# Two attention and feed-forward layers on one core: a repeated block for TensorE, other buffer slots, and the output projection at each layer's end

## The chip, the core and the metric

The kernel runs on one core of a Trainium2 chip. A core has TensorE (PE; its weight loads are shown as PEld), VectorE (DVE), ScalarE (ACT), GpSimd (POOL) and SyncE (SP), which here issues every transfer between HBM and SBUF. The engines run their own instruction streams and wait for each other on semaphores. The metric is the device time of one execution in microseconds; lower is better.

## The reference, cut to what matters

One decoding step of two layers that share their weights and their caches. B = 4 sequences, D = 512, 32 query heads in 8 groups of 4, head size 128, 8192 cached positions, feed-forward width 1792, all bfloat16.

```python
def _A_ref(x, k_cache, v_cache, wq, wo):
    q = (x @ wq)                                  # [B, 1, 32*128], by heads
    k, v = repeat(k_cache, 4), repeat(v_cache, 4) # 8 groups serve 32 heads
    scores = einsum("bhqd,bhkd->bhqk", q, k) * 128 ** -0.5
    p = softmax(scores)
    return einsum("bhqk,bhkd->bhqd", p, v) @ wo
def _B_ref(x, w_gate, w_up, w_down):
    return (silu(x @ w_gate) * (x @ w_up)) @ w_down
for _ in range(2):
    x = x + _A_ref(_layernorm(x), k_cache, v_cache, wq, wo)
    x = x + _B_ref(_layernorm(x), w_gate, w_up, w_down)
```

A cache of one sequence and group is 2 MB of keys and 2 MB of values. Both layers read all 32 of them.

## The kernel before

A *unit* is one pair of sequence and group; each layer has 32 (`NU`). SBUF holds eight slots of 2 MB (`NSLOT`) in the tensor `kvf`, and the weights `w_q` and `w_o` for good. The feed-forward weights are loaded into slots 6 and 7 (and some space behind them) at each layer's end. The last three units' keys and values of layer 1 stay in their slots, and layer 2 begins with them; so layer 2 loads 29 units.

**Transfers.** `items` lists them in order: keys of unit i, values of unit i-1, keys of unit i+1, and so on, with the parts of `w_o` in between at the start and the feed-forward weights at a layer's end. `pump` (L316) issues on SP whatever comes next while a slot is free; `finished` (L363) gives a slot back when TensorE's last read of it is written down. Any free slot may be taken. SP waits, in order, for the engines that used the slot last. In layer 2 two resident key slots are refilled in halves (`half`, L350).

**A unit.** The keys arrive with positions on partitions. `turn` (L396) lets VectorE transpose them 32 by 32 in place, in eight blocks of 128x512. `scores` (L414) multiplies each block with the placed query (`place_q`, L404, on GpSimd), four matmuls a block, into one PSUM bank. Then come a maximum (`max_p`, `max_t`, L425 to L439: VectorE, a transposing matmul, VectorE, ScalarE), the exponentials (`exps`, L441), a transposition of the probabilities (`turn_p`) and their sum (`total`). `values` (L496) multiplies the probabilities with the values in 16 matmuls of 512 columns; VectorE and ScalarE add up the diagonal blocks (`own_first`, `own_others`), a small matmul sums rows (`add_rows`, L535), and the result goes to `oT`. The last two units of a layer (`NLAST`) use 64 small matmuls instead (`block_last`, L540).

**The order.** Python code writes one order by hand for all engines: `keys` and `values` append blocks with an estimated length, `drain` keeps two microseconds of blocks behind the turns (`LAG`), and `line` and `after` hold the steps of the softmax and of the values, which `advance` lets out as time goes by. `_Sync` (L21) writes down who read and wrote what and puts a semaphore wait ahead of an instruction where needed.

**w_o.** When the four sequences of a group are done, `out_proj` (L575) is appended: 16 matmuls that gather the heads, a copy by VectorE, 16 matmuls with `w_o`, and the addition to x (`add_to_x`, L571). At a layer's end come the normalization (`center`, `deviation`), `ffn` (L647), and in the next layer `qproj` (L621).

TensorE's program is straight: every matmul of both layers stands in it, 4,700 in the built program.

Of the kernel before, what the change touches and what calls it, by code (L numbers as in the profile page):

```python
# [20 lines left out]
class _Sync:  # L21

    def __init__(self, engines, prog_sems):
        self.eng = engines
        self.prog = prog_sems
        self.count = {n: 0 for n in engines}
        self.waited = {}
        self.res = {}
        self.semval = {}

# [24 lines left out]
    def _wait(self, engname, need):  # L55
        e = self.eng[engname]
        for sem, val in need:
            k = (engname, id(sem))
            if self.waited.get(k, 0) >= val:
                continue  # L60
            if sem is self.prog.get(engname) and (val > self.count[engname] or engname == "pe"):
                continue
            e.wait_ge(sem, val)
            self.waited[k] = val

    def _record(self, engname, sv, reads, writes):
# [6 lines left out]
        for r in reads:  # L73
            rec = self.res.get(r)
            if rec is None:
                rec = self.res[r] = _Rec()
            rec.r[engname] = sv

# [25 lines left out]
def bass_interleave_layers__gqa_block_cached__swiglu_ffn__decode_kernel(  # L104
# [17 lines left out]
    REP = Hq // G  # L122
# [25 lines left out]
    with ExitStack() as es:  # L148
# [7 lines left out]
        o4 = sb("o4", [P, REP, B], BF16)  # L156
# [24 lines left out]
        xs = sb("xs", [P, B], FP32)  # L181
        vs = sb("vs", [P, B], FP32)
        lnv = sb("lnv", [P, B], FP32)
        rstd = sb("rstd", [P, B], FP32)
        oT = sb("oT", [P, 2, REP, B], BF16)
# [4 lines left out]
        zq = sb("zq", [P, 4, ZP + P], BF16)  # L190
# [99 lines left out]
        free = list(range(NSLOT))  # L290
        slot_of = {}

# [23 lines left out]
        def pump():  # L316
            while issued[0] < len(items):
                n = issued[0]
                it = items[n]
                if it[0][0] == "w":  # L320
                    if it[0] == "wg":
                        if not {NKEEP, NKEEP + 1} <= set(free):
                            return
                        free[:] = [s for s in free if s < NKEEP]
# [4 lines left out]
                late = any(e - 10 < n < e for e in ends)  # L329
                fit = [s for s in free if s < NKEEP or not late]  # L330
                if not fit:
                    return
                s = fit[0] if late else max(fit, key=lambda s: s >= NKEEP)
# [29 lines left out]
        def finished(it):  # L363
# [8 lines left out]
            else:  # L372
                free.append(slot_of[it])
# [22 lines left out]
        def turn(L, u, q):  # L396


            s = slot_of["K", L, u]
            w = kv[:, s, q * TB * Dh:(q + 1) * TB * Dh].bitcast(FP32)  # L400
            T.op("dve", lambda e: e.transpose(w, w), reads=[f"s{s}.{q}"], writes=[f"s{s}.{q}"])  # L401
            turned.add((L, u, q))

        def place_q(u, eng="pool", src=qr, keys_=SCR):  # L404
# [4 lines left out]
            dst = zq[:, :, ZP:].rearrange("p c (a x) -> p c a x", a=NA)[:, :, :, 0:REP]  # L409
# [4 lines left out]
        def scores(L, u, q):  # L414

            s = slot_of["K", L, u]
# [3 lines left out]
            for c in range(4):  # L420
                T.op("pe", lambda e: e.matmul(bank(bk)[:, 0:SW], lhsT=zq[:, c, z0:z0 + P], rhs=w[:, :, c // 2, :, c % 2],  # L421
                                              start=(q == 0 and c == 0), stop=(q == NB - 1 and c == 3)),
                     reads=[f"s{s}.{q}", "zq"], writes=[f"pb{bk}"], sig=(c == 3))
# [6 lines left out]
        def max_t(u):  # L430
            T.op("pe", lambda e: e.matmul(bank(STEP)[0:1, 0:P], lhsT=mx[:], rhs=identf[:], is_transpose=True,  # L431
                                          start=True, stop=True),
                 reads=["mx", "ident"], writes=[f"pb{STEP}"])
# [7 lines left out]
        def exps(u):  # L441
            bk = SBK[turn_of[u]]
            T.op("pe", lambda e: e.matmul(bank(STEP)[:, 0:1], lhsT=mrow,  # L443
                                          rhs=onesf[0:1, :], start=True, stop=True),
                 reads=["pb", "onesf"], writes=[f"pb{STEP}"])
# [10 lines left out]
        def total(u):  # L456
            T.op("pe", lambda e: e.matmul(bank(TOT)[:, 0:REP], lhsT=ones, rhs=rsm[:], start=True, stop=True),  # L457
                 reads=["rsm", "onesf"], writes=[f"pb{TOT}"])
# [4 lines left out]

        blocks = []
# [8 lines left out]
        def keys(L, u):  # L473
            def block(q):
                first = u == unit_order[L][0]
                if q == 0 and not first:
# [16 lines left out]

        done = set()

        def values(L, u):  # L496
            g, b = unit_gb(u)
            bk = OBK[turn_of[u]]

# [8 lines left out]
            def block(i):  # L508
# [5 lines left out]
                for t in range(TB):  # L514
                    j = t % NA
                    c0 = t * QB + i * NV * REP
                    T.op("pe", lambda e: e.matmul(bank(bk)[j * QB:j * QB + NV * REP, :],  # L517
                                                  lhsT=pT[:, turn_of[u], c0:c0 + NV * REP], rhs=v[:, t, NV * i:NV * (i + 1), :],
                                                  start=(i == 0 and t == j), stop=(i == 1 and t >= TB - NA)),
                         reads=[f"s{s}.{NV * i + k}" for k in range(NV)] + [f"pT{turn_of[u]}"], writes=[f"pb{bk}"],  # L520
                         sig=(t == TB - 1))
# [13 lines left out]
            def add_rows():  # L535
                T.op("pe", lambda e: e.matmul(bank(LNB)[:, 0:REP], lhsT=acc[:], rhs=head[:], start=True, stop=True),  # L536
                     reads=["acc", "head"], writes=[f"pb{LNB}"])
                scale_o(LNB)

            def block_last(q):  # L540
# [6 lines left out]
                for t in range(q * TB, (q + 1) * TB):  # L547
                    c0 = (t % TB) * QB + REP * q
                    T.op("pe", lambda e: e.matmul(bank(bk)[:, 0:REP], lhsT=kv[:, s, t * Dh:(t + 1) * Dh],  # L549
                                                  rhs=pT[:, turn_of[u], c0:c0 + REP], start=(t == 0), stop=(t == TT - 1)),  # L550
                         reads=[f"s{s}.{q}", f"pT{turn_of[u]}"], writes=[f"pb{bk}"], sig=(t % TB == TB - 1))
# [3 lines left out]
            def scale_o(k):  # L555
                T.op("dve", lambda e: e.tensor_tensor(oT[:, g // (G - 1), :, b], bank(k)[:, 0:REP], rl[:, rl_of[u], :],
                                                      ALU.mult),
                     reads=[f"pb{k}", f"rl{rl_of[u]}"], writes=[f"oT{g // (G - 1)}"])
# [8 lines left out]
            if all((L, g * B + k) in done for k in range(B)):  # L567
                rest.append([0.5, None, lambda: out_proj(g)])
# [6 lines left out]
        def out_proj(g):  # L575

            pick = ident.rearrange("p (j e) -> p e j", e=REP)
            ob = bank(OUTB)[:, XB:2 * XB].rearrange("p (e b) -> p e b", b=B)
            for c in range(REP):
                for h in range(REP):  # L580
                    T.op("pe", lambda e: e.matmul(ob[h * QB:(h + 1) * QB, c, :], lhsT=pick[:, c, :],
                                                  rhs=oT[:, g // (G - 1), h, :], start=True, stop=True),
                         reads=[f"oT{g // (G - 1)}", "ident"], writes=[f"pb{OUTB}"], sig=(h == REP - 1))
            T.op("dve", lambda e: e.tensor_copy(o4[:], ob), reads=[f"pb{OUTB}"], writes=["o4"])
            for nt in range(KT):
                for c in range(REP):
                    T.op("pe", lambda e: e.matmul(bank(OUTB)[:, nt * B:(nt + 1) * B],  # L587
                                                  lhsT=wo_sb[:, g, c, nt * P:(nt + 1) * P], rhs=o4[:, c, :],
                                                  start=(c == 0), stop=(c == REP - 1)),
                         reads=[f"wo{g // (G // 4)}", "o4"], writes=[f"pb{OUTB}"], sig=(c == REP - 1))  # L590
# [6 lines left out]
        def center():  # L597
            T.op("dve", lambda e: e.tensor_reduce(xs[:], xT[:].rearrange("p (k b) -> p b k", b=B), AX.X, ALU.add),
                 reads=["x"], writes=["xs"])
            T.op("pe", lambda e: e.matmul(bank(LNB)[:, 0:B], lhsT=ones, rhs=xs[:], start=True, stop=True),  # L600
                 reads=["xs", "onesf"], writes=[f"pb{LNB}"])
# [11 lines left out]
        def deviation(bias, bkey):  # L613
            T.op("pe", lambda e: e.matmul(bank(TOT)[:, 0:B], lhsT=ones, rhs=vs[:], start=True, stop=True),
                 reads=["vs", "onesf"], writes=[f"pb{TOT}"])
            T.op("act", lambda e: e.activation(lnv[:], bank(TOT)[:, 0:B], ACTF.Ln, scale=1.0 / D, bias=eps_sb[:]),
                 reads=[f"pb{TOT}", "eps"], writes=["lnv"])
            T.op("act", lambda e: e.activation(rstd[:], lnv[:], ACTF.Exp, scale=-0.5, bias=bias[:]),
                 reads=["lnv", bkey], writes=["rstd"])

        def qproj(gs, u=None):  # L621
            h0, nh = gs[0] * REP, len(gs) * REP
            for h in range(h0, h0 + nh):
                for kt in range(KT):
                    T.op("pe", lambda e: e.matmul(bank(LNB)[:, h * B:(h + 1) * B],  # L625
                                                  lhsT=wq_sb[:, kt, h * Dh:(h + 1) * Dh],
                                                  rhs=xn[:, kt * B:(kt + 1) * B],
                                                  start=(kt == 0), stop=(kt == KT - 1)),
# [7 lines left out]
            for c in range(4):  # L636
                for a in range(NA):
                    T.op("pe", lambda e: e.matmul(ob[a * QB:(a + 1) * QB, c, :, h0:h0 + nh],
                                                  lhsT=pick[:, c // 2, :, c % 2],
                                                  rhs=qT[:, :, h0:h0 + nh], start=True, stop=True),  # L640
# [6 lines left out]
        def ffn(last):  # L647
# [5 lines left out]
            for (w_sb, wname, bk) in (([wg_sb[:, k, :] for k in range(KT)], "wg", gb), (wu_sb, "wu", ub)):  # L653
                for fo in range(FO):
# [3 lines left out]
                    for kt in range(KT):  # L658
                        T.op("pe", lambda e: e.matmul(bank(bk)[:, fo * B:(fo + 1) * B],
                                                      lhsT=w_sb[kt][:, f:f + 2 * P - 1:2],  # L660
                                                      rhs=xn[:, kt * B:(kt + 1) * B],
# [99 lines left out]
```

## Time and profile before

| | us |
|---|---|
| median of 3 runs | 655.31 (654.31 to 655.44) |
| profiled execution | 655.51 |
| its span, first to last instruction | 653.7 |
| PE busy | 500.5 (77%) |
| DVE busy | 446.1 (68%) |
| ACT busy | 116.4 (18%) |
| HBM read | 273.88 MB, 419 GB/s over the span |
| TensorE's mean granted clock | 0.824 |

A row of the profile's groups gives the line, the engine, the operation, what it writes and reads, how often, the busy time with the mean of one in ns, and the idle time of the engine ahead of it with what ended it. In the 40 slices, one is 16.3 us, and a digit is a tenth of it. "DMA" there is the mean busy share of the core's 16 DMA engines. The queue "q8 instruction" carries TensorE's program to the engine while it runs. A transfer is split over all 16 DMA engines and has landed when the last of them has done its part.

### The profile page before, as it was taken

What the parts mean: (1) busy time and instruction counts of PE and PEld (TensorE: products, weight loads), DVE (VectorE), ACT (ScalarE), POOL (GpSimd) and SP (SyncE); (2) the same over time, 40 slices, a digit from 0 to 9 for tenths busy, and PEclk for the clock granted to TensorE, in tenths of its full rate; (3) what the DMA queues carried; (4) which work ended last, traced back from release to release, by engine and by line L of the source; (5) the groups of instructions that cost most, each with busy time, mean ns of one, the idle gap of its engine ahead of it and who ended that gap; (6) DMA issues with size and microseconds to landing.
All of it is one profiled execution on the core that took longest, in us unless ns stands there. A gap on an engine that the chain in (4) does not pass through costs nothing.

```text
span 653.7 us, 11807 instructions
## 1 busy us (share of the span) xinstructions
PE 500.5 (77%) x4896; PEld 319.2 (49%) x4896; DVE 446.1 (68%) x1079; ACT 116.4 (18%) x391; POOL 19.3 (3%) x73
## 2 busy tenths in 40 slices
PE   1766787977777877787876988887688787786886
PEld 1544444544444544544555655554354454443456
DVE  2556676776776777776752399996677677676682
ACT  0021121221221221221220212221122122121120
POOL 0000000000000000000000000000000000000000
PEclk9897788777978778789685989997978887797895
DMA  9999999999999999999999999999999999999996
GB/s 368 428 425 423 438 429 427 432 431 429 430 431 429 430 430 432 430 432 428 427 416 375 398 411 431 430 428 429 430 428 429 433 430 430 432 427 429 432 420 239
DMA packets 24085, 274.64 MB, mean 420 GB/s; under 512 B 2392, under 2 KB 2400, under 8 KB 7904
## 3 DMA queue, kind: packets, MB, share of 16 engines
q1 hardware_dynamic: 24032, 273.89, 98.9%
q8 instruction: 38, 0.62, 0.3%
q14 instruction: 15, 0.12, 0.0%
HBM read 273.88 MB, written 0.00 MB: 419 GB/s over the span
## 4 chain that ended last, share of the span: by engine, by line
DMA 66%; DVE 17%; PE 13%; SPq 3%; issue 1%; ACT 0%; POOL 0%; DVEq 0%; POOLq 0%
DMA kvf<-in_A_k_cache_dram 63%; DVE kvf L401 11%; PE ps L421 8%; DVE acc L531 3%; DMA kvf<-in_B_w_down_dram 3%; SPq L93 2%; PE ps L517 1%; DVE one L427 1%; DVE pT L454 1%; PE ps L587 1%; DVE m L434 1%; PE ps L625 1%; PE ps L457 0%; PE ps L676 0%; PE ps L549 0%
## 5 line engine op out<-in xcount | busy, mean ns | idle before, releaser
L401 DVE STREAM_TRANSPOSE kvf<-kvf 128x512 f32<-128x512 f32 x488 | 322.4, 686 | 121.8 <-DMA kvf<-in_A_k_cache_dram 121.8
L421 PE MATMUL ps<-kvf,zq 128*128 128x256 bf16 x2048 | 346.2, 314 | 18.2 <-DVE kvf L401 15.7
L421 PEld LDWEIGHTS ps<-kvf,zq 128*128 128x128 bf16 x2048 | 211.3, 115 | 89.8 <-DVE kvf L401 40.4
L437 ACT ACTIVATE pb<-m 1x128 f32<-1x128 f32 x64 | 19.7, 308 | 453.5 <-DVE m L434 453.5
L431 PE MATMUL ps<-identf,one 128*1 128x128 f32 x64 | 18.3, 286 | 68.3 <-DVE one L427 68.3
L517 PE MATMUL ps<-kvf,pT 128*16 128x512 bf16 x960 | 68.5, 409 | 0.9 <-DVE rl L459 0.9
L531 DVE SCALAR_TENSOR_TENSOR acc<-ps,own,acc 128x128 f32<-128x128 f32 x180 | 63.1, 351 | 6.5 <-ACT acc L526 1.9
L431 PEld LDWEIGHTS ps<-identf,one 128*1 128x1 f32 x64 | 5.1, 80 | 99.4 <-DVE one L427 93.2
L536 PE MATMUL ps<-head,acc 128*128 128x4 f32 x120 | 26.4, 290 | 17.9 <-DVE acc L531 17.7
L536 PEld LDWEIGHTS ps<-head,acc 128*128 128x128 f32 x120 | 22.8, 237 | 34.2 <-DVE acc L531 33.6
L443 PE MATMUL ps<-one,pb 1*128 1x1 f32 x128 | 27.8, 284 | 14.1 <-ACT pb L437 13.8
L443 PEld LDWEIGHTS ps<-one,pb 1*128 1x128 f32 x128 | 22.4, 217 | 32.8 <-ACT pb L437 29.1
L449 ACT ACTIVATE pb<-ps,one,rstd 128x256 bf16<-128x256 f32 x64 | 36.2, 565 | 2.1
L412 POOL TENSOR_TENSOR zq<-scr,quad 128x64 bf16<-128x64 bf16 x62 | 18.2, 293 | 608.1 <-PE ps L421 569.4
L517 PEld LDWEIGHTS ps<-kvf,pT 128*16 128x16 bf16 x960 | 19.3, 91 | 32.8 <-issue 21.2
L427 DVE TENSOR_REDUCE one<-ps 128x1 f32<-128x256 f32 x64 | 25.6, 399 | 13.1 <-PE ps L421 12.7
L454 DVE STREAM_TRANSPOSE pT<-pb 128x256 bf16<-128x256 bf16 x64 | 25.9, 405 | 1.9 <-ACT pb L449 1.9
L457 PEld LDWEIGHTS ps<-rsm,one 128*128 128x128 f32 x128 | 24.5, 237 | 3.0 <-ACT rsm L451 0.9
L457 PE MATMUL ps<-rsm,one 128*128 128x4 f32 x128 | 21.6, 239 | 0.0
L447 ACT ACTIVATE one<-ps,rstd 128x1 f32<-128x1 f32 x64 | 16.7, 261 | 25.8 <-PE ps L443 25.8
L526 ACT ACTIVATE acc<-ps,own 128x128 f32<-128x128 f32 x60 | 20.6, 343 | 0.0
L434 DVE TENSOR_REDUCE m<-ps 1x4 f32<-1x128 f32 x64 | 15.6, 244 | 6.5 <-PE ps L431 6.5
(66 smaller groups left out, 165.9 us busy)
## 6 DMA issues: line engine op xcount, KB each, us to landing
kvf<-in_A_k_cache_dram SPq DMA_DIRECT2D x60, 2048.0 KB, 30.0
kvf<-in_A_v_cache_dram SPq DMA_DIRECT2D x58, 2048.0 KB, 33.8
wq_sb<-in_A_wq_dram SPq DMA_DIRECT2D x4, 1024.0 KB, 7.6
wo_sb<-in_A_wo_dram SPq DMA_DIRECT2D x4, 1024.0 KB, 34.5
kvf<-in_A_v_cache_dram SPq DMA_DIRECT2D x8, 512.0 KB, 19.3
kvf<-in_B_w_gate_dram SPq DMA_DIRECT2D x2, 1792.0 KB, 23.2
kvf<-in_B_w_down_dram SPq DMA_DIRECT2D x4, 768.0 KB, 16.0
kvf<-in_A_v_cache_dram SPq DMA_DIRECT2D x2, 1024.0 KB, 7.0
```

The lines of the kernel that those rows point to most:

```text
L401: T.op("dve", lambda e: e.transpose(w, w), reads=[f"s{s}.{q}"], writes=[f"s{s}.{q}"])
L421: T.op("pe", lambda e: e.matmul(bank(bk)[:, 0:SW], lhsT=zq[:, c, z0:z0 + P], rhs=w[:, :, c // 2, :, c % 2], start=(q == 0 and c == 0), sto ...
L427: T.op("dve", lambda e: e.tensor_reduce(mx[:], bank(bk)[:, 0:SW], AX.X, ALU.max), reads=[f"pb{bk}"], writes=["mx"])
L431: T.op("pe", lambda e: e.matmul(bank(STEP)[0:1, 0:P], lhsT=mx[:], rhs=identf[:], is_transpose=True, start=True, stop=True), reads=["mx", " ...
L434: T.op("dve", lambda e: e.tensor_reduce(m4[:], bank(STEP)[0:1, 0:P].rearrange("p (x h) -> p h x", h=REP), AX.X, ALU.max, negate=True), rea ...
L443: T.op("pe", lambda e: e.matmul(bank(STEP)[:, 0:1], lhsT=mrow, rhs=onesf[0:1, :], start=True, stop=True), reads=["pb", "onesf"], writes=[f ...
L449: T.op("act", lambda e: e.activation(pb[:], bank(bk)[:, 0:SW], ACTF.Exp, bias=nm[:], scale=by, accum_out=rs[:]), reads=[f"pb{bk}", "nm", " ...
L454: T.op("dve", lambda e: e.transpose(pT[:, turn_of[u], :], pb[:]), reads=["pb"], writes=[f"pT{turn_of[u]}"])
L457: T.op("pe", lambda e: e.matmul(bank(TOT)[:, 0:REP], lhsT=ones, rhs=rsm[:], start=True, stop=True), reads=["rsm", "onesf"], writes=[f"pb{T ...
L517: T.op("pe", lambda e: e.matmul(bank(bk)[j * QB:j * QB + NV * REP, :], lhsT=pT[:, turn_of[u], c0:c0 + NV * REP], rhs=v[:, t, NV * i:NV * ( ...
L531: T.op("dve", lambda e: e.scalar_tensor_tensor(acc[:], bank(bk)[:, k * Dh:(k + 1) * Dh], own[:, k:k + 1], acc[:], op0=ALU.mult, op1=ALU.ad ...
L536: T.op("pe", lambda e: e.matmul(bank(LNB)[:, 0:REP], lhsT=acc[:], rhs=head[:], start=True, stop=True), reads=["acc", "head"], writes=[f"pb ...
```

## The change

TensorE's instructions are no longer issued as they are written down. `_Sync.pe` puts them on a list with the waits that they need, and `roll` at the end looks for the longest stretch in each layer where two units repeat with the same operands and with waits whose values grow evenly. That stretch becomes a loop of TensorE alone; its waits compare with register values worked out from the turn. In the built program the loops take units 2 to 27 of layer 1 (13 turns) and units 10 to 29 of layer 2 (10 turns), counted by their place in the layer; 2,388 matmuls are left in the program. `head_slot` asks that the loop's first instruction lie at the start of a block of instructions.

For the operands to repeat, each transfer has a fixed slot (`home`), and keys are turned into another slot (`turned_in`) except in the first two units of layer 1, the first ten of layer 2 (`CALM`) and the last units. The landing slot is given back when VectorE has turned the keys. In layer 1 keys land in slots 0 to 3 and are turned into 6 and 7, and values take 4 and 5. In layer 2 the first ten units use all eight slots; after them keys land in 7, 0, 1 and 6 and are turned into 2 and 3, and values again take 4 and 5.

The output projection of groups 0 to 2 is done at once ahead of the scores of unit 30, that of groups 3 to 5 ahead of unit 31's (and of group 6, in layer 1); the groups left over come as before. The copy between the two sets of matmuls is made by ScalarE there. `oT` holds all groups, `o4` up to three. `xs` and `lnv` are merged into `vs`, and `zq`'s four parts share their padding.

```diff
+    def play(self, ops, value=lambda sem, val: val):
+        e = self.eng["pe"]
+        for (out, lhsT, rhs), left, sig, kw in ops:
+            for sem, val in left:
+                e.wait_ge(sem, value(sem, val))
+            ins = e.matmul(out, lhsT=lhsT, rhs=rhs, **kw)
+            if sig:
+                ins.then_inc(self.prog["pe"], 1)
...
+        CALM = 10
+
+        def home(it):
+            kind, L, u = it
+            i = unit_order[L].index(u)
+            if L == 0:
+                if kind == "K":
+                    return NKEEP + i if i < 2 else (i - 2) % 4
+                return 2 if i == NU - 1 else 4 + i % 2
+            if kind == "K":
+                return 0 if i == NU - 1 else (7, 0, 1, 6)[i % 4]
+            return 2 if i == NU - 1 else (5, 4, 2, 3)[i % 4] if i < CALM else (5, 4)[i % 2]
+
+        def turned_in(L, u):
+            i = unit_order[L].index(u)
+            if i >= (NU - NRES, NU - 2)[L] or i < (2, CALM)[L]:
+                return slot_of["K", L, u]
+            return (NKEEP + i % 2, 2 + i % 2)[L]
...
-                s = fit[0] if late else max(fit, key=lambda s: s >= NKEEP)
+                s = home(it)
+                if s not in free:
+                    return
...
-            T.op("dve", lambda e: e.transpose(w, w), reads=[f"s{s}.{q}"], writes=[f"s{s}.{q}"])
+            s, to = slot_of["K", L, u], turned_in(L, u)
+            if q == 0 and to != s:
+                free.remove(to)
+            src, dst = (kv[:, k, q * TB * Dh:(q + 1) * TB * Dh].bitcast(FP32) for k in (s, to))
+            T.op("dve", lambda e: e.transpose(dst, src), reads=[f"s{s}.{q}"], writes=[f"s{to}.{q}"])
             turned.add((L, u, q))
+            if q == NB - 1 and to != s:
+                free.add(s)
+                pump()
...
+                if q == 0:
+                    tails.append(len(T.tape))
+                    at = L, unit_order[L].index(u)
+                    for gs in between.get(at, ()):
+                        project(gs, "act")
+                    heads.append(len(T.tape))
...
+        between = {(0, NU - 2): [[0, 1, 2]], (0, NU - 1): [[3, 4, 5], [6]],
+                   (1, NU - 2): [[0, 1, 2]], (1, NU - 1): [[3, 4, 5]]}
...
-            if all((L, g * B + k) in done for k in range(B)):
-                rest.append([0.5, None, lambda: out_proj(g)])
+            if (L, g) in late_g and all((L, g * B + k) in done for k in range(B)):
+                rest.append([0.5, None, lambda: project([g], "dve")])
...
+        def project(gs, eng):
+
+            n = len(gs)
             pick = ident.rearrange("p (j e) -> p e j", e=REP)
+            ob = bank(OUTB)[:, XB:XB + REP * n * B]
+            grid = ob.rearrange("p (e g b) -> p e g b", e=REP, b=B)
             for c in range(REP):
                 for h in range(REP):
+                    T.pe(grid[h * QB:(h + 1) * QB, c, :, :], pick[:, c, :], oT[:, gs[0]:gs[0] + n, h, :],
+                         reads=[f"oT{g}" for g in gs] + ["ident"], writes=[f"pb{OUTB}"], sig=(h == REP - 1),
+                         start=True, stop=True)
+            if eng == "dve":
+                T.op("dve", lambda e: e.tensor_copy(o4[:, 0:REP * n * B], ob), reads=[f"pb{OUTB}"], writes=["o4"])
+            else:
+                T.op("act", lambda e: e.activation(o4[:, 0:REP * n * B], ob, ACTF.Copy), reads=[f"pb{OUTB}"], writes=["o4"])
+            to = [(c, k) for k in range(n) for c in range(REP)]
             for nt in range(KT):
+                for c, k in to:
+                    T.pe(bank(OUTB)[:, nt * B:(nt + 1) * B], wo_sb[:, gs[k], c, nt * P:(nt + 1) * P],
+                         o4[:, (c * n + k) * B:(c * n + k + 1) * B],
+                         reads=[f"wo{gs[k] // (G // 4)}", "o4"], writes=[f"pb{OUTB}"], sig=((c, k) == to[-1]),
+                         start=((c, k) == to[0]), stop=((c, k) == to[-1]))
             add_to_x()
...
+                T.play(ops[at:heads[n]])
+                with nc.Fori(1, 1 + turns, 1, engines=(pe,), head_slot={pe: 0}) as i:
+                    value = {}
+                    for _, left, _, _ in body:
+                        for sem_, v in left:
+                            d, = step[id(sem_)]
+                            value[id(sem_), v] = nc.tensor.to_reg(i * d + (v - d))
+                    T.play(body, lambda sem_, v: value[id(sem_), v])
+                at = tails[n + 2 * turns]
+            T.play(ops[at:])
```

## The prediction, made before the changed kernel ran

> **What bounds the kernel now.** I read the page first (slices, queues, chain), then the waits, the chain at the layers' ends, the timeline there, and the trace's DMA packet records.
>
> ```profile
> DMA  9999999999999999999999999999999999999996
> GB/s 368 428 425 423 438 429 427 432 431 429 430 431 429 430 430 432 430 432 428 427 416 375 398 411 431 430 428 429 430 428 429 433 430 430 432 427 429 432 420 239
> q8 instruction: 38, 0.62, 0.3%
> ```
>
> The DMA engines are full from the second slice to the last but one. What can move the end is thus DMA time, the idle stretch at the layers' boundary (slices 21 to 24) and the tail (the last slice). The instruction queue looks like nothing, but it isn't spread evenly. In the packet records a 16 KB data packet takes 611 ns on its engine; an instruction packet takes 878 to 968 ns and slows the next data packet (1113 ns at 59.3). Each engine ends its share of a transfer with a 4-byte write, so the 16 writes show how far the engines lie apart: 0.62 us at 27 us, 1.87 after the first instruction packet, 3.80 at 327 us, 0.75 after the boundary's idle time, 3.53 at 434 us and 4.78 at 620 us. One instruction packet throws its engine back by 1.25 to 1.34 us, and a key or value unit has landed only with its last engine. The packets' durations repeat with period eight, and the ninth is the first that makes the spread jump again: eight engines take turns. The slowest has been hit two or three times in each layer.
>
> The chain that ended last, near the end:
>
> ```profile
> 587.74 32.59 DMA kvf<-in_A_k_cache_dram
> 620.35 0.71 DVE kvf L401
> 621.06 0.31 DVE one L427
> 621.37 1.21 DVE kvf L401 x2
> ...
> 633.79 0.97 PE ps L517 x16
> ...
> 640.58 0.55 issue
> 641.13 0.79 PE ps L549 x24
> ```
>
> From the landing of the keys of unit 30 of layer 2 (call it L = 620.3) on, no transfer is waited for by more than 0.2 us: the tail is a chain of VectorE and TensorE of 33.3 us. Layer 1's end is different; there TensorE waits for weights:
>
> ```profile
> 342.89 0.91 PE L659 MATMUL ps<-xn,kvf 128*128 128x4 bf16 x28 [0.94 <-DMA kvf<-in_B_w_gate_dram]
> 347.31 1.63 PE L659 MATMUL ps<-xn,kvf 128*128 128x4 bf16 x56 [2.34 <-DMA kvf<-in_B_w_up_dram]
> 351.04 1.07 PE L676 MATMUL ps<-scr,kvf 128*128 128x4 bf16 x32 [0.98 <-DMA kvf<-in_B_w_down_dram]
> ```
>
> **The change, part by part.** *The loop.* TensorE's built program goes from 4,700 matmuls to 2,388; units 2 to 27 of layer 1 are 13 turns, units 10 to 29 of layer 2 ten turns of one block. The page has 2 x 4896 TensorE instructions for 38 instruction packets, some 258 in each; a turn has about 220, so it fits one packet if it begins at a packet's start, which the loop asks for. By the counts of the straight parts, layer 1 then has some eight instruction packets before its last weights instead of 17, and layer 2 six or seven before the loop ends instead of 16. With eight engines taking turns, none is hit twice by then, and the spread stays near the 2.1 to 2.2 us that the trace shows at 126 and at 380 us. So the late landings come earlier by 3.80 - 2.1 = 1.7 us in layer 1, and L by 4.78 - 2.15 = 2.6 us in layer 2 (ends: 1.25, one hit less, and 4.2, no hit at all).
>
> [...]
>
> Each turn also has seven register and branch instructions. No row has one; the nearest are "issue" gaps on TensorE, 0.2 to 0.55 us each, so 1.5 to 3.9 us a turn, or nothing where the sequencer runs ahead. I take 1.5, hidden: with data there a unit takes 7.05 us (390.52 to 397.56 to 404.63 in the chain), and a unit's 4 MB come in 9.72 us, so two units have 5.3 us to spare. Without this cover, 23 turns would cost 35 us. Waits on registers go with it.
>
> *Slots.* Keys are turned out of place (the same 686 ns) and their landing slot is free after VectorE, not after the scores. Values have two slots in turn, so V(i+2) is issued when V(i) is used. The worst use so far comes 7.7 us after landing (77.86 to 85.58), and K(i+2), V(i+1), K(i+3), 14.6 us, are then queued: SP's queue does not run dry, and everything behind the waiting issue has 5 us of room. The tightest place is K31 of layer 2, which waits for K29 being turned: 7.2 us after landing, against 9.7 us until its turn; an issue on idle queues took 1.7 us to first data (349.02 to 350.7), which leaves 0.8. Layer 2's first ten units take the same slots' successors as before. Cost: zero; at worst 2 us.
>
> *w_o.* Before, a group costs TensorE about 1.5 us:
>
> ```profile
> 78.63 0.42 PE L581 MATMUL ps<-oT,identf 128*32 128x4 bf16 x16
> 79.59 0.57 PE L587 MATMUL ps<-o,wo_sb 128*128 128x4 bf16 x16 [0.54 <-DVE o L584]
> ```
>
> Six of these a layer lay under the DMA and were worth nothing. Now three groups at once stand ahead of the scores of units 30 and 31 (in layer 1 a seventh group too): 16 x 26 ns + 48 x 36 ns = 2.15 us, plus the copy. The copy moves to ScalarE, where it queues behind these:
>
> ```profile
> 621.54 1.12 PE L421 MATMUL ps<-kvf,zq 128*128 128x256 bf16 x8
> 622.77 0.31 ACT L437 ACTIVATE pb<-m 1x128 f32<-1x128 f32 x1 [7.43 <-DVE m L434]
> 622.99 0.34 ACT L526 ACTIVATE acc<-ps,own 128x128 f32<-128x128 f32 x1
> ```
>
> So in layer 2 the picks run at L + 1.4, the copy ends at L + 3.3, the 48 matmuls at L + 5.2, and unit 30's scores begin there instead of at L + 1.2: 4.0 us. VectorE's addition to x stands after its fourth turn (L + 3.1) and holds its queue until L + 5.4; behind it wait the three additions of unit 28 and the other turns. Scores of unit 30 end at 630.7 instead of 628.0 (all at the old L), since TensorE no longer waits for turns there. The second three groups take 2.7 us more, with VectorE waiting again 1.8 us, and V29 starts at 638.6 instead of 633.8. Followed to the end, V31 ends 4.5 to 5 us later; without the 0.55 us gap I take 4.5 (ends: 2.0, if all of TensorE's 3.7 us of idle time in 621 to 642 can be used against 5.7 us of work; 6.3, if none of it but the copy's wait).
>
> In layer 1 the same chain plus the seventh group (1.5 us and its wait for the addition) starts 1.3 us earlier, and a group of 1.5 us is gone from unit 29. V31 then ends at 343.4 instead of 339.3. Most of the 4.1 us is taken from the 0.56, 0.94 and 2.34 us for which TensorE waited for transfers, themselves 1.5 us earlier now: up projection ends at 349.7 instead of 348.9. The next keys' issue hangs on it (349.02 before), so layer 2's transfers start 0.7 us later (ends: 1.7 earlier, 1.5 later).
>
> **Sum.** -2.6 + 0.7 + 4.5 = +2.6 us on the span of 653.7, 656.3. The profiled run took 655.51 with that span, 0.2 above the median, 655.31; so 657.9.
>
> **The rivals.** *The tail hides it (faster).* The waits of TensorE for VectorE in 621 to 634 are used, the tail grows by 2.0, and layer 1's end, bound by weights, passes its 1.7 on: -2.6 - 1.7 + 2.0 = -2.3, 653.0. For it: 9.94 us of TensorE work in 12.3 us there. Against it: VectorE is busy 11.75 of the same 12.3, and the additions to x stop it. It decides where the tail grows by less than what the landings gain.
> *A balance (same).* Tail 3.3, boundary -0.4: +0.3, 655.6.
> *The loop saves no packets.* If each turn fetches again, two units cost one packet as now, the 2.6 is lost: 660.5. Against: the block fits and is aligned.
> *Starvation.* If values are used over 11 us after landing, the queue runs dry; five times 1 us on top of the forecast gives 662.9. Against: 7.7 now.
>
> **How the numbers follow.** Forecast 0.46 (own range 656 to 659.5), faster 0.24, balance 0.18, no packets saved 0.07, starvation 0.05. The range, 653.0 to 661.0, runs from the faster case to past the fourth. A difference under 0.2% (1.3 us) can't be told from none. Slower: 0.46 + 0.12, less 0.04 of the forecast that lies within 0.2%: 0.54. Same: 0.18 + 0.04 = 0.22. Faster: 0.24.
>
> **What would show it.** Instruction packets on q8 near 20; the spread of the closing writes 2.2 us, not 4.8, at unit 30's keys, and their landing near 618.4; 16 + 48 matmuls with a ScalarE copy between them after it, and V29's sixteen matmuls at L + 18 instead of L + 13.4; K3's issue near 349.7. Wrong if TensorE's scores of unit 30 start within 3 us of L, if V29 does within 16 us of it, if q8 stays near 38, or if the slices before the last fall below 425 GB/s.

## The result, and the profile after

The changed kernel takes 658.35 us (median of 17 runs, 656.73 to 661.24), the kernel before beside it 655.31 (654.31 to 657.05): a ratio of 1.0054, 95% interval 1.004 to 1.0068. It is slower by 3.0 us in the medians. The profiled execution took 657.94 us with a span of 656.2, against 653.7 before. The runs of the changed kernel also scatter more than those of the one before.

The page of the changed kernel, by slices of 16.4 us: TensorE's granted clock in tenths, the DMA engines' busy share, their rate; then the instruction queue with its packets.

```profile
PEclk9887789878878779779785979997877988787986
DMA  9999999999999999999997999999999999999995
GB/s 368 429 426 421 434 430 431 431 431 431 431 431 430 431 430 431 430 431 429 430 412 308 426 417 429 430 427 431 430 430 430 431 431 431 431 429 430 397 400 229
...
q8 instruction: 20, 0.33, 0.2%
```

The loop did what it says: 20 instruction packets instead of 38. Two things are worse than before. Slice 22, the boundary of the layers, fell from 375 to 308 GB/s, and slices 38 and 39, ahead of the tail, from 432 and 420 to 397 and 400.

The chain of waits at the end, by start, length, engine and line:

```profile
600.61 18.26 DMA kvf<-in_A_k_cache_dram
622.01 9.04 PE ps L96 x102
631.34 6.96 PE ps L96 x102
642.86 1.62 PE ps L96 x56
647.50 3.26 PE ps L96 x103
651.54 1.56 PE ps L96 x53
```

Unit 30's keys land at 618.86 (L). Before, VectorE's turns stood behind that landing; now TensorE stands there almost without a break (every matmul has line 96, since one function issues them all). The timeline shows the head of that chain, three groups of w_o at once:

```profile
620.19 0.42 PE L96 MATMUL ps<-oT,identf 128*32 128x12 bf16 x16
621.77 0.18 ACT L634 ACTIVATE o<-ps 128x48 bf16<-128x48 f32 x1
622.01 1.37 PE L96 MATMUL ps<-o,wo_sb 128*128 128x4 bf16 x48 [1.40 <-ACT o L634]
623.24 1.87 PE L96 MATMUL ps<-kvf,zq 128*128 128x256 bf16 x8
623.42 0.17 DVE L617 TENSOR_TENSOR xT<-xT,ps 128x16 f32<-128x16 f32 x1 [1.53 <-PE ps L96]
```

TensorE waits 1.40 us for ScalarE's copy, VectorE 1.53 us for the matmuls, and the scores of unit 30 begin at L + 4.4 (before: L + 1.2). From there to the values of unit 29 (623.24 to 637.05) TensorE stands still for only 0.32 us, where before it waited 2.3 us in all between the same two points. But its granted clock is 0.76 in that stretch, where before it was 1.00: the eight score matmuls above take 1.87 us, before 1.12.

At the end of layer 1 the waits for weights that the prediction showed are gone; these are the matmuls with the same weights now:

```profile
347.02 0.89 PE L96 MATMUL ps<-xn,kvf 128*128 128x4 bf16 x28 [0.36 <-DVE acc L657]
348.19 2.38 PE L96 MATMUL ps<-xn,kvf 128*128 128x4 bf16 x84
351.00 1.66 PE L96 MATMUL ps<-scr,kvf 128*128 128x4 bf16 x56 [0.43 <-DVE scr L717]
```

The weights lie there when TensorE comes to them, so it is the chain of TensorE and VectorE that sets when the layer ends.

With three landmarks the whole difference of the spans can be placed. Layer 2 loads keys from its unit 3 on; those of unit 6 land at 384.41 instead of 383.85: +0.56 from the boundary. From there to L it takes 234.45 us instead of 236.48: -2.03. From L to the end it takes 37.30 instead of 33.40: +3.90. The sum is +2.43.

### The profile page after: what moved, and what is told of

Read it like the earlier page. It is cut to its first block, busy times and chain, and to the rows that moved or that the text cites. A ratio compares the mean times of both kernels' runs of the same rounds, so it can differ in the third digit from the quotient of the medians.

```text
span 656.2 us, 11694 instructions
## 1 busy us (share of the span) xinstructions
PE 491.4 (75%) x4768; PEld 320.8 (49%) x4768; DVE 443.0 (68%) x1058; ACT 117.1 (18%) x396; POOL 19.3 (3%) x73
## 4 chain that ended last, share of the span: by engine, by line
DMA 54%; PE 21%; DVE 20%; SPq 2%; issue 2%; ACT 1%; POOL 0%; DVEq 0%; POOLq 0%
DMA kvf<-in_A_k_cache_dram 54%; PE ps L96 21%; DVE kvf L438 13%; DVE acc L577 3%; SPq L114 2%; DVE one L467 1%; DVE pT L492 1%; DVE m L473 1%; ACT pb L476 0%; ACT acc L572 0%; DVE oT L602 0%; DVE xT L617 0%; DVE scr L692 0%; DVE rl L497 0%; ACT o L634 0%
## 5 line engine op out<-in xcount | busy, mean ns | idle before, releaser
L96 PE MATMUL ps<-kvf,zq 128*128 128x256 bf16 x2048 | 343.3, 315 | 33.0 <-issue 16.8
L96 PE MATMUL ps<-kvf,pT 128*16 128x512 bf16 x960 | 64.1, 388 | 2.1 <-DVE rl L497 2.1
L96 PEld LDWEIGHTS ps<-one,pb 1*128 1x128 f32 x128 | 24.1, 234 | 29.1 <-ACT pb L476 17.8
L96 PEld LDWEIGHTS ps<-head,acc 128*128 128x128 f32 x120 | 24.8, 256 | 24.9 <-DVE acc L577 23.4
L96 PE MATMUL ps<-one,pb 1*128 1x1 f32 x128 | 29.6, 298 | 9.8 <-ACT pb L476 9.7
L489 ACT ACTIVATE rsm<-head,one 128x4 f32<-128x4 f32 x64 | 19.0, 297 | 2.1
```

Of the source, the lines that this page charges most:

```text
L96: ins = e.matmul(out, lhsT=lhsT, rhs=rhs, **kw)
L489: T.op("act", lambda e: e.activation(rsm[:], head[:], ACTF.Copy, scale=rs[:]), reads=["head", "rs"], writes=["rsm"])
```

## The experiments

Times are medians of 5 to 17 runs; a ratio is that to the kernel before, run beside it. The runs were made on several chips, so ratios compare better than times. "First keys" is the issue of layer 2's first keys, "middle" the time from the landing of unit 6's keys to L, "tail" that from L to the end of the span.

| run | us | ratio, 95% | first keys | middle | tail |
|---|---|---|---|---|---|
| before | 655.31 | 1 | 349.02 | 236.48 | 33.4 |
| changed | 658.35 | 1.0054, 1.004 to 1.0068 | 350.65 | 234.45 | 37.3 |
| e5_changed_again | 659.13 | 1.0049, 1.0033 to 1.0065 | 352.81 | 234.94 | 37.3 |
| e1_straight | 659.52 | 1.0053, 1.0033 to 1.0073 | 352.65 | 235.23 | 37.0 |
| e2_slots_only | 656.76 | 1.0023, 1.0008 to 1.0037 | 349.02 | 237.65 | 34.1 |
| e12_slots_k31 | 656.17 | 1.001, 0.9998 to 1.0023 | 348.93 | 236.01 | 33.1 |
| e3_wo_early | 658.42 | 1.0046, 1.0029 to 1.0063 | 348.18 | 234.82 | 39.0 |
| e4_k31_slot | 654.59 | 0.999, 0.9979 to 1.0 | 348.03 | 234.22 | 34.6 |
| e8_early_straight | 655.30 | 1.0005, 0.9993 to 1.0016 | 349.01 | 235.25 | 33.2 |
| e6_changed_k31_slot | 659.28 | 1.0056, 1.0037 to 1.0075 | 352.67 | 235.27 | 37.5 |
| e10_l1_early | 656.26 | 1.0018, 1.0009 to 1.0026 | 347.93 | 234.86 | 36.4 |
| e7_body_across | 657.20 | 1.0035, 1.0023 to 1.0046 | 352.54 | 235.40 | 37.2 |
| e9_kept_busy | 659.76 | 1.0062, 1.0049 to 1.0075 | 350.80 | 236.86 | 37.5 |
| e11_shifted | 654.01 | 0.9979, 0.9968 to 0.9989 | 348.04 | 235.42 | 33.9 |

**The loop away.**

```diff
-        roll()
+        T.play(T.tape)
```

> The changed kernel, but TensorE's program is written out in full, without the repeated block; slots and w_o stay as changed. Theory (the loop gives back time through fewer instruction packets): about 37 packets on the instruction queue instead of 20, the closing writes of unit 30's keys in layer 2 spread over 4 to 5 us instead of 2.5, these keys land 3.2 us later after the restart, and the time is that of the changed kernel, 658.4, plus 3.2: 661.5 us (660.5 to 662.5). Rival one (the loop saves nothing): 658.4. Rival two (the loop itself costs time, 0.73 us of issue in each of 23 turns showing through): below 658, down to 650 if none of it were covered.

The packets are back (37), but the time is 659.52, some 0.4 to 1.2 us over the changed kernel's two medians, with intervals of the ratios that cover each other: under the theory's range, and nearer the first rival. The second, that the loop itself costs, falls. The closing writes of unit 30's keys lie 3.35 us apart, not 4 to 5: twice as many packets don't bring back the 4.78 of the kernel before.

**The slots alone.**

```diff
-        between = {(0, NU - 2): ...}
+        between = {}
-        roll()
+        T.play(T.tape)
```

> The new slots and the turning of keys out of place alone: no repeated block, and each group's w_o spread over the layer as before. Theory (the slots are nearly free): within 0.9 us of the kernel before, 655.3 to 656.2; the 0.9 is the dip in transfers between 615 and 620 us while the last keys wait for a slot, which makes the values of unit 30 land late for a tail that is as quick as before. Rival (the slots starve the queue through the layers, and are what the change costs): 657.5 or more, with slices below 425 GB/s in the middle of the layers.

656.76, a ratio of 1.0023: the slots aren't free, and both the theory's bound (656.2) and the rival's (657.5) are missed. Slice 38 is at 347 GB/s: the keys of unit 31 were issued at 619.02, when unit 29's had been turned, and the middle one of their 16 closing writes comes 8.05 us after that of unit 30's keys, where 4.9 us lie between other units.

**w_o two units earlier, then the slot of the last keys.**

```diff
-        between = {(0, NU - 2): [[0, 1, 2]], (0, NU - 1): [[3, 4, 5], [6]],
-                   (1, NU - 2): [[0, 1, 2]], (1, NU - 1): [[3, 4, 5]]}
+        between = {(0, NU - 4): [[0, 1, 2]], (0, NU - 3): [[3, 4, 5]], (0, NU - 1): [[6]],
+                   (1, NU - 4): [[0, 1, 2]], (1, NU - 3): [[3, 4, 5]]}
...
-                last = L * NU + NU - 1
+                last = L * NU + min([i for l, i in between if l == L])
```

> The changed kernel with the six groups of w_o two units earlier in both layers (groups 0 to 2 before unit 28, 3 to 5 before unit 29; group 6 of layer 1 stays where it was); layer 2's repeated block then has 9 turns, not 10. Theory (what w_o costs is its place at the ends): the first matmul of unit 30's scores comes about 1.2 us after its keys land (4.4 in the changed kernel), the end 33.4 to 34.4 us after that landing (37.3), layer 2's first keys are issued 1 to 2.5 us earlier than 350.65, and the time is 651 to 653.5 us, faster than both kernels. Rival one (the w_o costs TensorE and VectorE the same wherever it stands): 658.4. Rival two (the loop or the slots cost the time): 656 or more.

The first keys of layer 2 are issued at 348.18, 2.5 us earlier, as expected; the time is 658.42, as the rivals have it. The timeline of this run shows why, at the values of unit 30:

```profile
632.52 0.27 PE L96 MATMUL ps<-identf,one 128*1 128x128 f32 x1
635.85 0.95 PE L96 MATMUL ps<-pT,kvf 128*128 128x4 bf16 x32 [3.05 <-DMA kvf<-in_A_v_cache_dram]
```

and its rates:

```profile
GB/s 368 430 427 421 440 431 431 431 431 431 431 431 430 433 431 431 430 431 429 429 410 351 413 421 431 429 430 432 431 431 429 432 431 431 431 431 430 327 403 241
```

TensorE is early now, and waits 3.05 us for values that come late: slice 38 is at 327 GB/s. The engines ran out of transfers because the keys of unit 31 were issued only at 617.31: VectorE's addition to x waits 1.51 us for w_o's matmuls ahead of unit 29's last turns, which now end 9.3 us after the landing of unit 29's keys (7.0 in the changed kernel). The next run exchanges the landing slots of units 27 and 29, so that the slot for the last keys is free two units earlier:

```diff
-                return 0 if i == NU - 1 else (7, 0, 1, 6)[i % 4]
+                return 0 if i >= NU - 5 and i % 4 == 3 else 6 if i == NU - 3 else (7, 0, 1, 6)[i % 4]
```

> As the run with w_o two units earlier, and the last keys of layer 2 get a landing slot whose keys were turned two units before, so that their transfer does not wait for VectorE. Theory (the dip at 615 to 620 us starves what a quick tail waits for next, the values of unit 30): the slices at the end of layer 2 stay above 425 GB/s and the time is 0.5 to 1.0 us below the run without this change. Rival (the dip lies under TensorE's work): the same time within 0.3 us.

The same two lines of its page and timeline:

```profile
GB/s 370 430 420 426 440 426 430 432 433 434 430 426 431 434 433 432 426 429 433 431 412 371 397 422 431 430 426 431 433 433 427 431 429 432 433 430 432 426 421 239
```

```profile
631.94 0.27 PE L96 MATMUL ps<-identf,one 128*1 128x128 f32 x1
632.17 0.95 PE L96 MATMUL ps<-pT,kvf 128*128 128x4 bf16 x32
```

Slice 38 is at 426, the wait is gone, and the time is 654.59: 3.8 us from the exchange of two slots, nearly four times the most that was expected.

**The changed kernel again, with that slot, and with its block across two packets.**

```diff
-                with nc.Fori(1, 1 + turns, 1, engines=(pe,), head_slot={pe: 0}) as i:
+                with nc.Fori(1, 1 + turns, 1, engines=(pe,), head_slot={pe: 128}) as i:
```

> The changed kernel as it is, for comparison on one chip with the three runs beside it. All theories: 658.4 us (657 to 659.5), ratio 1.003 to 1.007.

> The changed kernel, w_o at the layers' ends and all, with the one slot of the run e4_k31_slot: the last keys of layer 2 no longer wait for VectorE. Theory (w_o at the end holds TensorE back so far that the hole in the transfers at 615 to 620 us lies under it: the values of unit 30 landed 3.5 us and the gate weights 2.2 us before they were used): within 0.8 us of the changed kernel, the end still 37 us after unit 30's keys. Rival (the hole is what the change costs, as it cost the run with w_o earlier 3.8 us): 654 to 655.5 us.

> The changed kernel with one number altered: the repeated block begins 128 instructions after a packet's start, so that its 216 or so instructions lie in two packets. Theory one (a branch back to the packet before has to be fetched anew): 23 to 46 packets more on the instruction queue than the 20 of the changed kernel, the closing writes of unit 30's keys 4 us or more apart, and 1 to 3 us more than the changed kernel. Theory two (both packets stay in reach): 20 to 22 packets, and the changed kernel's time within 0.7 us.

The exchange that was worth 3.8 us is worth nothing where w_o stands at the end (659.28 beside 659.13): its theory holds. The block across two packets has 20 packets too, so it isn't fetched anew in each turn. Its time, 657.2, was expected by neither theory; its interval overlaps that of the changed kernel beside it, and whether it is faster stays open. That the block has to lie in one packet to be loaded once was the prediction's assumption (its reason against the rival in which the loop saves no packets); with 20 packets either way, these runs don't bear it out.

The profiled execution of e5_changed_again took 660.49, 2.55 more than that of the same program above, and 2.06 of it are there when the keys of unit 6 of layer 2 land. The two traces differ at layer 1's end in the granted clock, the third number from the end here; first the changed kernel's first execution, then the second:

```profile
318.00:344.00 26.00, 21.89 (x387) 17.29 (x387) 15.94 (x40) 5.54 (x20) 0.29 (x1) 0.79 1.01 416
```

```profile
318.00:344.00 26.00, 22.03 (x322) 16.49 (x322) 15.48 (x38) 5.56 (x20) 0.29 (x1) 0.74 1.01 417
```

By single microseconds the clock is 0.50 or 1.00, but for those in which it changes. The same eight matmuls show it in the timelines, of the first execution, where the half rate ends at 326, and of the second, where it lasts from 322 to 328:

```profile
325.87 1.13 PE L96 MATMUL ps<-kvf,zq 128*128 128x256 bf16 x8
```

```profile
325.75 1.87 PE L96 MATMUL ps<-kvf,zq 128*128 128x256 bf16 x8
```

Ahead of these rows the two run alike (w_o's first 48 matmuls begin at 321.16 and 321.08); behind them the values of unit 29 begin at 337.77 and 339.98, 2.2 us apart. The mean clock of 0.79 goes with first keys issued at 350.65, and 0.74 with 352.81; e1, e6 and e7 have 0.74 with 352.54 to 352.67. Before, the clock was 1.00 from 321 to 337 us, and what slowness it had before that (0.50 from 311 to 320) lay under the transfers, for which TensorE still waited 0.94, 2.34 and 0.98 us at the layer's end. With w_o at the end TensorE sets the boundary, so its clock is in the time. In two executions of one program the half rate thus fell at other times (319 to 326 us, 322 to 328); what sets them isn't shown.

**TensorE kept busy at the ends.**

```diff
+        def fill(k, n):
+            for i in range(n):
+                T.pe(bank(k)[:, 256:512], ident, wq_sb[:, 0, 0:256], reads=["ident", "wq0"], writes=[f"pb{k}"],
+                     sig=(i == n - 1), start=True, stop=True)
+
         def max_t(u):
+            if u == unit_order[len(heads) > NU][NU - 3]:
+                fill(OUTB, 16)
...
+            if len(gs) == 3 and 0 in gs:
+                fill(LNB, 12)
             if eng == "dve":
```

> The changed kernel with matmuls that nobody reads put into two waits of TensorE at each layer's end: 16 of 128x256 (some 1.7 us at the full clock) where it waits 2.2 us for the keys of unit 30, and 12 (1.3 us) between the picks and the matmuls of w_o, where it waits 1.5 us for ScalarE's copy. The products of the kernel stay the same; only work is added. Theory (the idle stretch and the small matmuls of w_o make the granted clock fall to 0.5 for the scores behind them): the clock stays near 1.0 from 616 to 630 us, eight score matmuls take 1.04 us instead of 1.87, the values of unit 29 are begun 15 to 16.5 us after unit 30's keys instead of 18.2, the runs scatter less than 656.7 to 661.2, and the time is 655 to 657.5 us against 658.4 to 659.1. Rival (what w_o costs is its work and its waits, at any clock): 658.4 to 660, the values of unit 29 still at 18 us.

The clock did what was wanted: 0.99, 1.00 and 0.88 from 620 to 635, where the changed kernel has 0.80, 0.52 and 1.00. But the values of unit 29 begin at L + 17.6, and the tail is 37.5 us: nearer the rival than the theory. The test isn't clean, since the added matmuls hold w_o's first 48 back from L + 3.15 to L + 3.8, and a gap of 0.64 us stands near the end. Between the first scores of unit 30 and the values of unit 29 it is 12.6 us instead of 13.8. So the clock is worth some 1.2 us of the tail here, less than the theory said, which leaves w_o's work and waits for the larger part. The time, 659.76, can't be used for either, because something else went wrong at the entry of layer 2's loop. The rows are the matmuls around it, then the loop's entry branch in this run and in the changed kernel, whose middle figure gives how long it took, in ns:

```profile
429.07 0.27 PE L96 MATMUL ps<-identf,one 128*1 128x128 f32 x1
434.59 1.67 PE L96 MATMUL ps<-kvf,zq 128*128 128x256 bf16 x7 [5.25 <-issue]
```

```profile
L774 PEldq COMPARE_BRANCH  x1: 5107/5107/5107, 428.8 to 428.8; - x1
```

```profile
L765 PEldq COMPARE_BRANCH  x1: 288/288/288, 428.4 to 428.4; - x1
```

TensorE stood for 5.25 us, 5.1 of them in this branch, with instruction packets at 431.5 and 437.5; slice 27 fell to 374 GB/s, and "middle" is 2.4 us longer than in the changed kernel. Of the added matmuls 28 stand in layer 1, ahead of that branch. The trace shows that the branch stood, not what it waited for.

**One layer at a time, and the loop away from the best order.** The first of these runs has the new entries of `between` for layer 1 alone, the second `T.play(T.tape)` in place of `roll()`, both with the slots exchanged.

> The changed kernel with the slot of the run e4_k31_slot and with layer 1's groups of w_o two units earlier, layer 2's still at its end: one half of the way from the run e6_changed_k31_slot (659.3) to e4_k31_slot (654.6). Theory one (both ends cost, layer 1's 2.6 to 4.6 us by the issue of layer 2's first keys, 350.65 to 352.7 against 348.03): first keys issued near 348, end still 37 us after unit 30's keys, 655.5 to 657 us. Theory two (the tail is the whole price, the boundary is taken up by later waits): 658 or more.

> The run e4_k31_slot (w_o two units earlier, the last keys' slot free in time) without the repeated block. Theory (the block saves packets, and with them 1 to 3 us of late landings): 37 or 38 packets, the closing writes of unit 30's keys 3.5 to 5 us apart instead of 3.0, and 655.6 to 657.6 us against 654.6. Rival (the block saves nothing that the end sees): 654.6 within 0.5 us.

Layer 1's w_o earlier (and the slots exchanged): 656.26, as its first theory says, from 659.28. Layer 2's too: 654.59. So w_o's place costs 3.0 us at the boundary and 1.7 in the tail (2.5 and 1.8 by the ratios). Without the loop the same order takes 655.30, with the closing writes 3.68 us apart against 3.05. That is 0.7 us for the loop (0.0015 of the ratio, 1.0 us), between the ranges of its theory and its rival, and the intervals of the two ratios overlap: a gain is likely, but not shown.

**The packets' bounds in the tail moved.** In e4_k31_slot TensorE stood between two of w_o's matmuls:

```profile
639.38 0.45 PE L96 MATMUL ps<-o,wo_sb 128*128 128x4 bf16 x11 [0.28 <-DVE o L632]
641.15 0.30 PE L96 MATMUL ps<-o,wo_sb 128*128 128x4 bf16 x5 [1.31 <-issue]
```

```diff
         def max_t(u):
+            if len(heads) > NU and u == unit_order[1][NU - 2]:
+                fill(OUTB, 64, 4)
```

The third argument of `fill` is the width here.

> The run e4_k31_slot with 64 matmuls of four columns that nobody reads, put where TensorE waits 2.4 us in the tail (624.3 to 626.75), which moves the bounds of the instruction packets behind them by half a packet. Theory (the 1.31 us of issue that TensorE waits at 639.84 are a packet that comes late, and its place is luck): the gap moves or vanishes, and the time lies up to 1.3 us below 654.6. Rival (the gap is something else, or the end waits for the weights anyway): 654.6 within 0.5 us, a gap of over 1 us at the same matmul of w_o.

```profile
641.60 0.59 PE L96 MATMUL ps<-o,wo_sb 128*128 128x4 bf16 x16 [0.28 <-DVE o L639]
```

The sixteen run in one piece and the tail is 33.9 us instead of 34.6. The time is 654.01, 0.58 below, with intervals of the ratios that overlap: the gap is gone, and what that is worth isn't clear of the noise. The ratio, 0.9979 (0.9968 to 0.9989), makes this the one version that is clearly faster than both kernels: by 0.2% against the one before and by 0.7% against the changed one (the quotient of the two ratios).

**The slots alone, with the last keys' slot mended.**

> The run e2_slots_only (new slots alone, TensorE's program in full, w_o spread over the layer; 656.8 us, ratio 1.0023) with the one slot of the run e4_k31_slot. Theory (what the slots cost is the one hole before the last keys, 8.05 us between closing writes instead of 4.9): no step over 5.5 us there, and 655.0 to 655.9 us, ratio 0.999 to 1.001. Rival (the slots cost elsewhere, at the change from ten units in one plan to the next near 430 to 440 us, where a slice of that run shows 414 GB/s): 656.3 us or more, ratio 1.0015 or above.

Slice 38 is at 430 and the long step is gone. 656.17 lies just above the theory's range and just below the rival's, the ratio (1.001) on the theory's bound. The hole was some 0.9 us (0.0013; 0.6 by the medians) of the slots' price, with intervals that overlap; up to 0.0023 may remain and isn't placed. The exchange is worth less here than the 3.8 us with w_o two units earlier, and the traces suggest why: in e2_slots_only the DMA engines lay 5.35 us apart ahead of the hole and 0.73 behind it, so the engine that was behind caught up while the others stood. The values of unit 30 landed at 636.46 with the hole and at 635.16 without it; with w_o earlier it was 635.80 and 632.13.

## Why the prediction was right

The time came out as predicted (657.9 against 658.35), for about half of the reasons given, and by errors that cancel. By its steps:

- *w_o in the tail, +4.5.* The mechanism is right: the 16 + 48 matmuls, ScalarE's copy and the values of unit 29 at L + 18.2 (said: 18). The size, 3.9 in the changed kernel's trace, is in part luck. The scores of unit 30 begin earlier than said (L + 4.4, not 5.2) and end later (L + 11.8, not 10.4), because the granted clock was at its half rate from 623 to 630 us and the term was reckoned at the full one. In the time, moving w_o is worth 1.7 to 2.3 us (e10_l1_early to e4_k31_slot and e11_shifted), since TensorE then stands elsewhere.
- *The layers' boundary, +0.7.* The term that was most too small: +1.6 at the first keys' issue in one execution, +3.8 in another, and 3.0 us of the time in e10_l1_early (2.5 by the ratios). The step took most of 4.1 us of w_o out of TensorE's waits for weights and reckoned TensorE at full clock; where it sets the boundary, the clock's half rate is added (the mean from 318 to 344 us was 0.79 and 0.74 in the two executions).
- *The loop, -2.6.* L came 1.47 earlier and 3.1 after the restart's delay of 1.63 is taken off (2.0 from the landing of unit 6's keys on, where only 0.56 of the delay is left), and the spread at unit 30's keys was 2.5 us (said: 2.2), which looks like a hit. The runs say otherwise: with loop and without, in the same order, the difference is 0.7 us. What failed is taking the 4.78 us of the kernel before (4.93 when the 16 writes are counted transfer by transfer, as here) for the spread of any straight program. Where w_o is spread over the layer straight programs have 5.35 (e2_slots_only) and 5.03 (e12_slots_k31), but in the order of the changed kernel it is 3.35 (e1_straight), and 3.68 in e8_early_straight. Layer 1's gain of 1.7 didn't come at all at unit 30's keys (317.92 against 317.95); its weights landed 0.9 to 1.0 us earlier. The step put the spread down to TensorE's packets, but with none of them between 42.4 and 304.5 us it is 3.46 at these keys, against 3.77 before (the last section shows with what it rose).
- *Slots at zero, with 0.8 us of margin for the last keys.* The price was wrong, and the margin is where it failed. The keys of unit 31 were issued 7.0 us after those of unit 29 had landed, as said (7.2). But the 9.7 us against it run to the last of the 16 closing writes of unit 30's keys; the first came at 616.38, 2.5 us earlier and only 0.2 us after the issue at 616.18. So engines stood without data (243 GB/s from 616.2 to 618.9), and slices 38 and 39 fall under the 425 GB/s that were to show the prediction wrong (slice 39 had 420 before, too). It cost nothing here (e6_changed_k31_slot) because w_o held TensorE back for longer; uncovered it costs 0.6 to 0.9 us with w_o spread over the layer (not clear of the noise) and 3.8 us with w_o two units earlier, where the keys are issued later still. The starvation rival named the right kind of fault, at the keys instead of the values.
- *The loop's own instructions, 1.5 us a turn, hidden.* The page gives 16.8 us of issue ahead of the scores, 0.73 for each of 23 turns; hidden, as said.

In sum by the pairs of runs, in ratios: w_o's place 0.0066 (e6_changed_k31_slot to e4_k31_slot), the loop -0.0015, the slots 0.001 (e12_slots_k31; the hole ahead of the last keys is hidden here), together 0.0061 or 4.0 us, against the 0.0054 or 3.5 us measured. By the medians it is 4.4 to 4.7 against 3.0. Of these only w_o's place is clear of the noise; with runs that scatter over 4 us the rest isn't placed. A boundary and slots that were priced too low stood against a loop priced too high.

The faster rival had TensorE's waits for VectorE used up by w_o, and they were: 0.32 us of them are left of 2.3. It failed all the same, because TensorE waited for the copy first (1.40 us) and then ran at half clock (0.52 on the mean from 625 to 630 us), and because the landings gained less than it counted on: 2.0 us, not 2.6, from the landing of unit 6's keys to L, and nothing at the boundary, where it had 1.7. The argument against it, that VectorE leaves these waits unusable, isn't what the trace shows.

## What to carry to other kernels

In this kernel w_o was hidden in the steady part of a layer, under the transfers, and had a price at the layers' ends, where TensorE, which does it, sets the time: 3.0 us at the boundary and 1.7 in the tail. Such work is worth moving in by two units; then look what starves next, since the same exchange of slots was worth nothing with the end held up and 3.8 us without. A gain that is read from one execution's pattern (which engine fell back how often) should be counted as luck until another program of the same kind shows it.

## What the runs showed of the hardware

- Not only TensorE's packets set the DMA engines apart: in the changed kernel, with none on q8 between 42.4 and 304.5 us, the spread of the closing writes still rose from 1.87 (180 us) to 2.75 (201) and 3.59 (279), in step with the 8 KB packets of q14 at 194.3, 198.6, 271.1 and 277.2. The page calls q14 an instruction queue; it has 15 packets in both kernels, and it is taken here for the other engines' programs.
- Among the small matmuls of the tail TensorE stood with nothing to wait for that the traces show: for 1.08 and 1.54 us in e3_wo_early, 1.31 in e4_k31_slot, and 0.55 from 640.58 us on in the kernel before, where q8 had an instruction packet from 639.0 to 640.0; in e11_shifted, with 64 small matmuls more ahead of them, not at all. That the instructions come late is the author's reading; no trace shows it.
- The branch at the entry of layer 2's loop took 0.29 us in the changed kernel and 5.1 us in e9_kept_busy; the branches back, one a turn, took 0.21 us each.
- In all six runs with w_o at layer 2's end and no added matmuls, the granted clock falls to half for 6.8 us that begin 2.3 to 4.1 us after L; the first eight score matmuls of unit 30 take 1.87 us there. Of the seven runs without w_o there, six have the full rate from L to L + 11 (1.04 to 1.23 us for eight), and one (e12_slots_k31) has a half rate in it. With the added matmuls (e9_kept_busy) it stays at full rate until L + 12. So where the half rate falls in the tail is hardly chance. That TensorE's waits bring it about fits the last of these, but that is one execution.
- Two executions of one program differed by 2.55 us, 2.06 of it there by the landing of unit 6's keys in layer 2, behind the stretch in which the half clock lay at other times (a mean of 0.79 and 0.74 from 318 to 344 us).
